# Some constants made on GpSimd, and each output chunk stored by one transfer instead of two

## The chip, the cores and the metric

The kernel runs on one core of a Trainium2 chip. The core has five engines with instruction queues of their own: TensorE (PE in the profile, with its weight loads as PEld), VectorE (DVE), ScalarE (ACT), GpSimd (POOL) and SyncE (SP), and 16 DMA engines that the queues of SP, ACT and GpSimd share. The metric is the device time of one execution in microseconds (us). One execution was also taken by the profiler; its span is the time from the first to the last recorded work on the core.

## The reference

The reference is a Nystromformer attention followed by a multiplicative feed-forward layer. All inputs are fp32.

```
A  = sm(q, k_lm); Bm = sm(q_lm, k_lm); C = sm(q_lm, k)      # 8 batches, 8 heads, 576 x 64; 32 landmarks
Z  = Bm^T / (norm1 * norminf);  six times: Z = 2 Z - Z Bm Z
x  = (A Z C v), heads side by side                           # 4608 x 512
h  = (x @ w1) * (x @ w2) @ w3                                # 512 -> 1024 -> 1024
out = h @ w_out                                              # 4608 x 512
```

`sm` is a softmax over the last axis with the scale 1/8, and `q_lm`, `k_lm` are means over groups of 18 rows.

## The kernel before

**Stages.** At the start w3 and w_out are folded into one matrix `w34` (8 row blocks of 128 x 512), each fp32 operand split into a high and a low fp16 part (`fold`, line 505: `split` makes the parts of w_out, `turn` transposes pieces of w3 on PE, `product` multiplies). Then each batch goes through its landmarks, the three score matrices, the inverse, and a projection of `Z C v` through w1 and w2 per head (`project`). `up` (line 451) multiplies this by the normalised scores and forms the product `ab` of the two branches, 128 of the 1024 features at a time. `down` (line 470) multiplies `ab` by `w34`: one chunk of 128 output rows is eight matmuls into the PSUM tile `acc`, and there are 36 chunks, nine for each pair of batches.

**Order.** The order is written out by hand in the string `ORDER`: words are run from left to right, and what each issues is queued on its engines in that order. `F` is one step of the fold, `U..` is `up`, `W0.n` and `W1.n` are the two halves of output chunk n. Waits come from the tiles: a tile that is used in rotation can be written again when its last readers are done.

**The output.** When chunk n is complete, ACT scales it from PSUM into `o_sb` (line 499; 128 x 512 fp32, three buffers in rotation), and SP sends it out in two transfers of 64 partitions (line 502). The rows of a batch are laid out as 64 positions x 9 phases: token 9 p + r of batch b is `rows[b, r, p]`. A unit of 64 partitions is one phase r of one batch, its 64 rows lie 9 rows apart in memory, and a chunk is two units that follow each other: mostly two phases of one batch, and in one chunk of nine the last phase of one batch and the first of the next. The last chunk (n = 35) is computed in two halves of 256 columns, each with an ACT or DVE evacuation (lines 481 and 484) and two transfers, one on SP and one on ACT (line 489). SP's queue also carries the loads of V (lines 126 and 131), the exchange of landmarks between partitions (line 232) and, at the start, pieces of w3 (line 574) and of w_out (line 578).

**The constants.** `constants` (line 162) is called once at the start, after GpSimd was given a copy that waits for a piece of w_out (`gate`, line 603) and eight load issues (lines 107 and 137). It makes, all on DVE: `mask4`, `eye`, `onesq`; `selc`, the 0/1 matrix with which PE spreads the softmax reciprocals over the columns (line 382); `lomask`; `eye2`; `bt`, whose second half holds the identity, used for the squares in line 305; and `xsp`, two zeroed tiles into which line 355 writes the landmark values. On GpSimd the next instruction behind the load issues is the copy in `paced_w3` (line 619), which lets SP send the fifth piece of w3 only once the first batch's k has come.

Of the kernel before, what the change touches and what calls it, by code (L numbers as in the profile page):

```python
# [21 lines left out]
DM = 512  # L22
# [4 lines left out]
RT = 9  # L27
# [40 lines left out]
def kernel(  # L68
# [11 lines left out]
    nc = tc.nc  # L80
# [8 lines left out]
    def big():  # L89
        return psp.tile([128, 2, 512], FP32, name="big", bufs=3)  # L90
# [4 lines left out]
    def acc():  # L95
        return psp.tile([128, 512], FP32, name="acc", bufs=1)
# [58 lines left out]
    for a in range(2):  # L155
        for x in range(2):
            sl = slice(64 * a + 32 * x, 64 * a + 32 * x + 32)
            for ph in range(2):
                c = 64 * a + 32 * ph
                nc.gpsimd.tensor_copy(out=pick[sl, x, c:c + 32], in_=ident[sl, sl])  # L160

    def constants():

        mask4 = consts.tile([128, 4, 32], FP32, name="mask4")
        eye = consts.tile([128, 2, 32], FP32, name="eye")
        onesq = consts.tile([128, 2, 4, 2, 4], FP16, name="onesq")
        nc.vector.memset(mask4, 0.0)
        nc.vector.memset(onesq, 0.0)
        for h in range(4):
            sl = slice(32 * h, 32 * h + 32)  # L170
            nc.vector.memset(mask4[sl, h, :], 1.0)
            for qd in range(2):
                nc.vector.tensor_copy(out=eye[sl, qd, :], in_=ident[sl, sl])
                nc.vector.memset(onesq[sl, qd, :, qd, h:h + 1], 1.0 / X64)

        selc = consts.tile([128, 2, 4, 128], FP16, name="selc")
        lomask = consts.tile([128, 1], FP32, name="lomask")
        selr = consts.tile([128, 8], FP32, name="selr")
        nc.vector.memset(selc, 0.0)
        nc.vector.tensor_tensor(out=selr, in0=eye[:, 0, 0:8], in1=eye[:, 0, 8:16], op=ALU.add)  # L180
        nc.vector.reduce_sum(out=lomask, in_=eye[:, 0, 8:16], axis=AX.X)
        nc.vector.tensor_scalar(out=lomask, in0=lomask, scalar1=-1.0, scalar2=None, op0=ALU.mult)
        for c in range(4):
            sl = slice(32 * c, 32 * c + 32)
            for qd in range(2):
                nc.vector.tensor_copy(
                    out=selc[sl, qd, c, :].rearrange("p (h m) -> p h m", m=32),
                    in_=selr[sl, 4 * qd:4 * qd + 4].unsqueeze(2).to_broadcast([32, 4, 32]),
                )
        eye2 = consts.tile([128, 32], FP32, name="eye2")  # L190
        nc.vector.tensor_tensor(out=eye2, in0=eye[:, 0], in1=eye[:, 0], op=ALU.add)
        bt = consts.tile([128, 4, 64], FP32, name="bt")
        for i in range(4):
            nc.vector.tensor_copy(out=bt[:, i, 32:64], in_=eye[:, 0])
        xsp = [consts.tile([128, 256], FP32, name=f"xsp{i}") for i in range(2)]
        for t in xsp:
            nc.vector.memset(t, 0.0)
        return mask4, eye, eye2, onesq, selc, lomask, bt, xsp


# [265 lines left out]
    rows = out.rearrange("(b p r) f -> b r p f", b=B, r=RT)  # L466

    hold = {}

    def down(n, half):  # L470
        b0, t0 = n // 9 * 2, 128 * (n % 9)
        ab = sts[b0]["ab"]
        if n == 35:
            o_sb = hold["o_sb"] = hold.get("o_sb") or po.tile([128, DM], FP32, name="o_sb")
            c = slice(256 * half, 256 * half + 256)
            pso = acc() if half else big()[:, 0, :]
            for j in range(8):
                nc.tensor.matmul(pso[:, 0:256], ab[:, j, t0:t0 + 128], w34[:, j, c],
                                 start=(j == 0), stop=(j == 7))
            if half == 0:  # L480
                nc.scalar.activation(out=o_sb[:, c], in_=pso[:, 0:256], func=AXF.Copy,
                                     scale=1.0 / (X64 * X64))
            else:
                nc.vector.tensor_scalar(out=o_sb[:, c], in0=pso[:, 0:256],
                                        scalar1=1.0 / (X64 * X64), scalar2=None, op0=ALU.mult)
            for i in range(2):
                u = t0 // 64 + i
                eng = nc.scalar if i else nc.sync
                eng.dma_start(out=rows[b0 + u // RT, u % RT][:, c], in_=o_sb[64 * i:64 * i + 64, c])
            return  # L490
        if half == 0:
            hold["ps"] = big()[:, 0, :] if n > 30 and n % 2 else acc()
        pso = hold["ps"]
        for j in range(4 * half, 4 * half + 4):
            nc.tensor.matmul(pso[:, :], ab[:, j, t0:t0 + 128], w34[:, j, :],  # L495
                             start=(j == 0), stop=(j == 7))
        if half == 1:
            o_sb = po.tile([128, DM], FP32, name="o_sb")
            nc.scalar.activation(out=o_sb, in_=pso, func=AXF.Copy, scale=1.0 / (X64 * X64))  # L499
            for i in range(2):  # L500
                u = t0 // 64 + i
                nc.sync.dma_start(out=rows[b0 + u // RT, u % RT], in_=o_sb[64 * i:64 * i + 64, :])


    def fold(pf, wof, w3f, wsp, warm_up):
# [102 lines left out]
    load_weight(0, moe_w1)  # L608
    load_weight(1, moe_w2)
    mask4, eye, eye2, onesq, selc, lomask, bt, xsp = constants()  # L610
    fd = fold(pf, wof, w3f, wsp, warm_up)
    next(fd)
# [43 lines left out]
    for word in ORDER.split():  # L656
        name, _, b = word.partition(".")
        if name == "F":
            next(fd, None)
        elif name == "P":  # L660
            paced_w3(int(b))
        elif name == "L3":
            load_w3(int(b))
        elif name[0] == "W":
            down(int(b), int(name[1]))
        else:
            b = int(b)
            if name == "U0a":
                if pab is None:
                    for _ in fd:  # L670
                        pass
                    pf_scope.__exit__(None, None, None)
                    pab = ctx.enter_context(tc.tile_pool(name="pab", bufs=2))
                open_ab(b)
            of_batch[name](sts[b], b)
# [30 lines left out]
```

## Time and profile before

| | us |
|---|---|
| median of three runs | 263.78 (263.65 to 267.96) |
| the profiled execution | 263.62 |
| its span | 261.8 |
| first and last chunk evacuated (line 499) | 86.5, 255.9 |
| last matmul ends | 257.59 |
| last store issued on SP | 258.38 |

The page of the profile gives, for each engine, its busy time and share of the span, then the chain of work that ended last, followed back from the end, and then groups of equal instructions with the mean duration of one. A row of the timeline reads: start and duration in us, engine, line and operation, output<-input, shape, count, and in brackets the idle time before it and what ended that. In the list of DMA issues the last number is the median time from issue to landing. Packets are what the DMA engines move one after the other; "under 512 B" counts all packets smaller than that.

### The profile page before, as it was taken

What the parts mean: (1) busy time and instruction counts of PE and PEld (TensorE: products, weight loads), DVE (VectorE), ACT (ScalarE), POOL (GpSimd) and SP (SyncE); (2) the same over time, 40 slices, a digit from 0 to 9 for tenths busy, and PEclk for the clock granted to TensorE, in tenths of its full rate; (3) what the DMA queues carried; (4) which work ended last, traced back from release to release, by engine and by line L of the source; (5) the groups of instructions that cost most, each with busy time, mean ns of one, the idle gap of its engine ahead of it and who ended that gap; (6) DMA issues with size and microseconds to landing.
All of it is one profiled execution on the core that took longest, in us unless ns stands there. A gap on an engine that the chain in (4) does not pass through costs nothing.

```text
span 261.8 us, 10518 instructions
## 1 busy us (share of the span) xinstructions
PE 251.5 (96%) x4578; PEld 148.7 (57%) x4578; DVE 173.8 (66%) x352; ACT 134.7 (51%) x305; POOL 103.2 (39%) x134
## 2 busy tenths in 40 slices
PE   7999999998989999999999999999999999999993
PEld 3455554454556558557654674766476556656642
DVE  8765887556958687788856958767775656464410
ACT  4543236343652565576449546746646555455531
POOL 3630018998981999027092597504400000000000
PEclk9999999999999999999999999999999999999999
DMA  6999998999963448976668496933640713222355
GB/s 236 333 243 284 245 248 191 183 137 240 175 105 50 120 101 167 216 195 114 131 100 162 101 214 150 161 58 86 147 86 3 173 43 80 45 62 61 81 118 127
DMA packets 25070, 37.78 MB, mean 144 GB/s; under 512 B 4672, under 2 KB 13120, under 8 KB 25024
## 3 DMA queue, kind: packets, MB, share of 16 engines
q1 hardware_dynamic: 14704, 24.65, 36.9%
q0 software_dynamic: 9728, 11.54, 28.1%
q10 hardware_dynamic: 592, 0.92, 1.1%
q8 instruction: 36, 0.59, 1.0%
q14 instruction: 10, 0.08, 0.1%
HBM read 38.80 MB, written 9.44 MB: 184 GB/s over the span
## 4 chain that ended last, share of the span: by engine, by line
PE 89%; DVE 4%; ACT 3%; issue 1%; DMA 1%; SPq 0%; DVEq 0%; ACTq 0%
PE big L455 23%; PE acc L495 22%; PE acc L530 14%; PE big L442 5%; PE big L344 5%; PE big L399 4%; PE big L517 2%; PE small L530 2%; PE big L382 2%; PE small L421 2%; PE big L274 1%; PE big L495 1%; PE big L322 1%; DVE ab L461 1%; PE small L248 1%
## 5 line engine op out<-in xcount | busy, mean ns | idle before, releaser
L455 PE MATMUL big<-ahat,gt 128*128 128x288 f16 x512 | 73.1, 287 | 0.7 <-DVE ab L461 0.6
L495 PE MATMUL acc<-w,ab 128*128 128x512 f16 x264 | 67.2, 380 | 0.0
L461 DVE TENSOR_TENSOR ab<-a_sb,big 128x576 f16<-128x576 f16 x64 | 48.0, 750 | 27.2 <-ACT a_sb L459 16.8
L455 PEld LDWEIGHTS <-gt 128*128 128x128 f16 x512 | 48.3, 98 | 21.1 <-issue 3.1
L459 ACT CAST a_sb<-big 128x576 f16<-128x576 f32 x64 | 40.8, 640 | 33.9 <-PE big L455 32.9
L206 POOL TENSOR_TENSOR tr<-qkT 128x1024 f32<-128x1024 f16 x14 | 29.7, 2123 | 70.0 <-DVE qkT L143 69.8
L530 PE MATMUL acc<-wsp,w3t 128*128 128x512 f16 x168 | 41.3, 380 | 0.7 <-ACT w L533 0.5
L495 PEld LDWEIGHTS <-ab 128*128 128x128 f16 x280 | 25.3, 98 | 24.9 <-issue 3.5
L499 ACT ACTIVATE o_sb<-acc 128x512 f32<-128x512 f32 x33 | 19.8, 599 | 19.5 <-PE acc L495 19.1
L530 PEld LDWEIGHTS <-w3t 128*128 128x128 f16 x192 | 18.1, 98 | 18.9 <-issue 1.3
L143 DVE STREAM_TRANSPOSE qkT<-qkn 128x576 uint32<-128x576 uint32 x32 | 24.0, 763 | 2.0 <-DMA qkn<-in_k_dram 2.0
L448 DVE TENSOR_SCALAR gt<-big 128x1024 f16<-128x1024 f32 x16 | 19.1, 1211 | 3.1 <-PE big L442 3.0
L446 ACT ACTIVATE gt<-big 128x1024 f16<-128x1024 f32 x16 | 15.9, 1032 | 5.9 <-PE big L442 5.9
L211 POOL TENSOR_TENSOR tr<-tr 128x512 f32<-128x512 f32 x14 | 17.9, 1282 | 0.6
L442 PE MATMUL big<-wup,zt 64*32 64x512 f16 x512 | 17.4, 380 | 0.2 <-ACT en L282 0.2
L523 DVE SCALAR_TENSOR_TENSOR w3t<-big,w3t 128x512 f16<-128x512 f32 x16 | 11.0, 687 | 10.0 <-ACT w3t L522 10.0
L522 ACT ACTIVATE w3t<-big 128x512 f16<-128x512 f32 x16 | 9.5, 596 | 13.9 <-PE big L517 13.8
L284 DVE STREAM_TRANSPOSE ent<-en 128x576 f32<-128x576 f32 x16 | 12.1, 768 | 4.4 <-ACT en L282 4.4
L344 PE MATMUL big<-vt,ent 64*32 64x64 f32 x1152 | 14.2, 226 | 0.0
L282 ACT ACTIVATE en<-big 128x288 f32<-128x288 f32 x32 | 12.7, 411 | 2.9 <-PE big L274 2.7
L344 PEld LDWEIGHTS big<-vt,ent 64*32 64x32 f32 x1152 | 12.7, 105 | 2.0 <-ACT a_sb L459 0.5
L328 ACT ACTIVATE eat<-big 128x576 f16<-128x576 f32 x16 | 9.6, 652 | 7.3 <-PE big L322 7.3
(214 smaller groups left out, 285.2 us busy)
## 6 DMA issues: line engine op xcount, KB each, us to landing
out_dram<-o_sb SPq DMA_DIRECT2D x70, 128.0 KB, 2.5
vt<-in_v_dram SPq DMA_DIRECT2D x16, 288.0 KB, 5.3
vt<-in_v_dram SPq DMA_DIRECT2D x32, 144.0 KB, 4.0
qkn<-in_k_dram POOLq DMA_DIRECT2D x12, 288.0 KB, 5.4
qkn<-in_q_dram POOLq DMA_DIRECT2D x12, 288.0 KB, 4.9
w3f<-in_moe_w_dram SPq DMA_DIRECT2D x6, 512.0 KB, 6.7
wup<-in_moe_w_dram POOLq DMA_DIRECT2D x4, 512.0 KB, 25.3
wof<-in_moe_w_out_dram SPq DMA_DIRECT2D x6, 256.0 KB, 4.5
```

Source lines behind the costliest of these rows:

```text
L143: nc.vector.transpose(out=st["qkT"][:, t, prs].rearrange("p c r q e -> p (c r q e)").bitcast(U32), in_=st["qkn"][:, t, prs, :].rearrange(" ...
L206: add(out=tr, in0=x[:, :, 0:4, :], in1=x[:, :, 4:8, :], op=ALU.add)
L211: add(out=tr[:, :, 0:2, :], in0=tr[:, :, 0:2, :], in1=tr[:, :, 2:4, :], op=ALU.add)
L344: nc.tensor.matmul(psV[32 * o:32 * o + 32, qd, 0:64], ent[sl, pr, r, :], vt[sl, pr, 64 * r:64 * r + 64], start=(r == 0), stop=(r == RT - 1 ...
L442: nc.tensor.matmul(psG[o:o + 32, qd, :], zt[rs, i, h, :], wup[rs, h, w, fs], start=(i == 0), stop=(i == 1), tile_position=(64 * qd, o))
L448: nc.vector.tensor_scalar(out=g[:, :, w, fs], in0=psG, scalar1=1.0 / ZS, scalar2=None, op0=ALU.mult)
L455: nc.tensor.matmul(p[:, c, 0:HS], st["g"][:, qd, w, 128 * j:128 * j + 128], st["ahat", qd][:, c, :], start=(qd == 0), stop=(qd == 1))
L459: nc.scalar.copy(out=st["a_sb"], in_=p[:, :, 0:HS])
L461: nc.vector.tensor_tensor(out=st["ab"][:, j, st["t0"]:st["t0"] + S].rearrange("p (c s) -> p c s", c=2), in0=st["a_sb"], in1=p[:, :, 0:HS], ...
L495: nc.tensor.matmul(pso[:, :], ab[:, j, t0:t0 + 128], w34[:, j, :], start=(j == 0), stop=(j == 7))
L499: nc.scalar.activation(out=o_sb, in_=pso, func=AXF.Copy, scale=1.0 / (X64 * X64))
L530: nc.tensor.matmul(psW[j][:, :], turned[j, c // 4][:, a, c % 4, :], wsp[:, b, c, :], start=(c == 0 and a + b == 0), stop=(c == 7 and a == 1))
```

## The change

`selc` is zeroed and filled on GpSimd instead of DVE, and so are the identity half of `bt` and the zeros of `xsp`; `selr`, `lomask` and `eye2` stay on DVE. The instructions are the same in kind and number, and stand on GpSimd behind the load issues and ahead of the copy of line 619.

The stores go through a new function `store`. Where both units of a chunk belong to one batch, one transfer takes all 128 partitions of `o_sb` and writes two phases of 64 rows (31 chunks). Where the chunk crosses from one batch to the next, two transfers of 64 partitions stay as they were (four chunks). The last chunk is stored in one transfer for each half of its columns, the first on ACT and the second on SP. In the built program the combined transfer has 128 x 512 elements on the side of `o_sb` and 2 x 64 x 512 on the side of the output, with steps of 512, 4608 and 1 element.

```diff
-        nc.vector.memset(selc, 0.0)
+        nc.gpsimd.memset(selc, 0.0)
...
-                nc.vector.tensor_copy(
+                nc.gpsimd.tensor_copy(
                     out=selc[sl, qd, c, :].rearrange("p (h m) -> p h m", m=32),
                     in_=selr[sl, 4 * qd:4 * qd + 4].unsqueeze(2).to_broadcast([32, 4, 32]),
                 )
...
         for i in range(4):
-            nc.vector.tensor_copy(out=bt[:, i, 32:64], in_=eye[:, 0])
+            nc.gpsimd.tensor_copy(out=bt[:, i, 32:64], in_=eye[:, 0])
...
         for t in xsp:
-            nc.vector.memset(t, 0.0)
+            nc.gpsimd.memset(t, 0.0)
...
+    def store(b, u, o_sb, c, eng):
+        bu, r = b + u // RT, u % RT
+        if r < RT - 1:
+            eng.dma_start(out=rows[bu, r:r + 2][:, :, c], in_=o_sb[:, c])
+            return
+        for i in range(2):
+            eng.dma_start(out=rows[bu + i, (r + i) % RT][:, c], in_=o_sb[64 * i:64 * i + 64, c])
...
-            for i in range(2):
-                u = t0 // 64 + i
-                eng = nc.scalar if i else nc.sync
-                eng.dma_start(out=rows[b0 + u // RT, u % RT][:, c], in_=o_sb[64 * i:64 * i + 64, c])
+            store(b0, t0 // 64, o_sb, c, nc.sync if half else nc.scalar)
...
-            for i in range(2):
-                u = t0 // 64 + i
-                nc.sync.dma_start(out=rows[b0 + u // RT, u % RT], in_=o_sb[64 * i:64 * i + 64, :])
+            store(b0, t0 // 64, o_sb, slice(0, DM), nc.sync)
```

## The prediction

> **What bounds the kernel now.** I read the head of the page first (busy shares), then the chain that ended last, then the DMA part, because half of the change is about stores.
>
> ```profile
> span 261.8 us, 10518 instructions
> ...
> PE 251.5 (96%) x4578; PEld 148.7 (57%) x4578; DVE 173.8 (66%) x352; ACT 134.7 (51%) x305; POOL 103.2 (39%) x134
> ...
> DMA packets 25070, 37.78 MB, mean 144 GB/s; under 512 B 4672, under 2 KB 13120, under 8 KB 25024
> ...
> PE 89%; DVE 4%; ACT 3%; issue 1%; DMA 1%; SPq 0%; DVEq 0%; ACTq 0%
> ...
> out_dram<-o_sb SPq DMA_DIRECT2D x70, 128.0 KB, 2.5
> ```
>
> PE is busy 96% of the span and makes 89% of the chain; DMA has 1% of the chain, the last store. So today nothing done to stores or to constants can win more than a few tenths, but anything that holds PE up is lost time in full. The 70 stores land in 2.5 us each (median) with the output buffer `o_sb` three deep, and a chunk is made every 4.9 us (36 chunks from 86.5 to 257.6 us), so they are far from PE.
>
> The number that I use most is "under 512 B 4672". Before has 196 transfers: 74 stores, 48 of V, 24 exchanges of landmarks, 18 of w3 and w_out, 32 on GpSimd. The exchanges move rows of 256 B, 24 x 64 = 1536 packets. What is left is 4672 - 1536 = 3136 = 196 x 16: each transfer leaves 16 tiny packets, one per DMA engine that took part. **Every transfer of before is cut over 16 engines**, and in each of them the outermost count is 32, 64 or 128 on both sides.
>
> **Part 1, constants.** The start, by the timeline:
>
> ```profile
> 3.14 0.48 DVE L179 MEMSET selc<- 128x512 uint32 x1 [0.15 <-issue]
> ...
> 3.98 1.45 DVE L186 CAST selc<-selr 32x128 f16<-32x128 f32 x8
> ...
> 5.55 0.43 DVE L194 COPY bt<-eye 128x32 f32<-128x32 f32 x4
> ...
> 5.98 0.55 DVE L197 MEMSET xsp<- 128x256 f32 x2
> ...
> 7.72 1.19 PE L530 MATMUL acc<-wsp,w3t 128*128 128x512 f16 x4 [0.22 <-DVE w3t L523]
> ...
> 17.75 0.18 POOL L619 CAST w3f<-qkn 128x1 f32<-128x1 f16 x1 [2.60 <-PE acc L530]
> ...
> 29.25 0.60 PE L517 MATMUL big<-ident,w3f 128*128 128x128 f32 x4
> ```
>
> DVE loses 0.48 + 1.45 + 0.43 + 0.55 = 2.91 us ahead of its first w_out split, which then starts when its input is there (5.34 us) and not at 6.44. PE's only wait on that is the 0.22 us in the row above; before and after it PE works off its own queue. Gain: 0 to 0.2, I take 0.2.
>
> GpSimd gets 15 instructions, behind its eight load issues, which end at 15.15 us. Bounds from its own rows: a 256-element fp16 memset takes 0.31 us and a 128-element fp32 one 0.20, so the memset of 1024 is about 0.97; a 32x32 cast takes 0.20 (1.58 / 8), and 96 elements more cost up to 0.21 by the two-input rate of L211 and L212 (2.15 ns an element), so eight are 1.6 to 3.3; four copies 0.8, two memsets 0.6: 4.0 to 5.7 us, 4.8 in the middle. The pacing copy L619 behind them moves from 17.75 to about 20.0, and with it the fifth 512 KB piece of w3, which SP issues at 17.96 and which takes some 6.7 us to land: 26.9 instead of 24.7. PE transposes that piece at 29.25. Cost 0, with 2.3 us of cover; beyond that it would cost PE us for us, once. The next GpSimd work (38.44) and the first readers of bt (40.2), xsp (60.4) and selc (62.3) are further off.
>
> **Part 2, stores.** 74 issues become 41: 31 of 256 KB and 8 of 128 KB on SP, and two of 128 KB for the last chunk, one on ACT, one on SP. Issuing is shorter (0.57 us each), which only matters at the very end: the last matmul ends at 257.59, DVE's piece at 258.11, and SP sends its second half-piece at 258.38; with one issue it leaves at 258.13. Gain 0.2 to 0.5.
>
> But the new store names its destination as 2 row phases x 64 rows x 512 elements, against 128 partitions on the other side. For the first time a transfer has an outermost count below 16. No row of before shows such a one; the bounds are 16 engines, as all others have, and 2. A cut along the outermost index fits all 196 transfers, and a cut along the flattened rows fits them too. I take 2: dividing the first dimension that an instruction lists is the simpler of the two, and every engine's share in before (2 to 8 whole outermost rows) can be had that way. This is a choice and not a reading, hence the weight of the first rival below.
>
> The Trainium skill, "DMA: Bandwidth & Descriptors", section "Why a DMA increments its semaphore by 16 and not by 1", says that a transfer runs on the largest number of engines up to 16 that divides the slowest dimension of both sides; by it the store runs on 2. The trace agrees as far as it goes (16 for 32, 64 and 128). The same page of the Trainium skill, in "Rules for kernel authors", asks for one 128-partition transfer in place of two halves, which speaks for the change; by that alone the time would be the first rival's.
>
> Price of a 256 KB store on two engines: 64 packets of 2 KB each. Two rows price a packet:
>
> ```profile
> 8.00:9.00 1.00, 1.00 (x6) 0.37 (x5) 1.00 (x3) 0.50 (x1) 0.00 (x1) 1.00 1.05 404
> ```
>
> (window; last two columns are the DMA share of 16 engines and GB/s): loads of full 128 partitions run at 404 / (16 x 1.05) = 24.0 GB/s per engine, 85 ns a packet. And for stores alone, from 210 to 256 us:
>
> ```profile
> DMA packets 1935, 3.26 MB, mean 71 GB/s; under 512 B 384, under 2 KB 384, under 8 KB 1928
> ...
> q1 hardware_dynamic: 1928, 3.16, 32.1%
> ```
>
> 0.321 x 46 us x 16 = 236 us over 1544 data packets, 153 ns. There sixteen engines pull from 64 partitions at once; the trace's packet records have the first packets of such a burst at 81 to 91 ns. Two engines, each on its own 64 partitions, don't crowd like that, so I take 85 and keep 153 as the other end. A store then holds its two engines 64 x 85 ns = **5.4 us** (up to 9.8), where chunks come every 4.9 us and in the tail every 1.7.
>
> Those two engines also carry their sixteenth of all loads. From 86 to 207 us (the loads end there) the three large queues hold 40.4 + 21.1 + 1.4% of 16 engines, 76 us per engine; stores are 41 x 64 x 153 ns / 16 = 25 of it, loads 51.
>
> The sum for one of the two engines from the first store on (87.1 us): 31 x 5.44 = 168.6; eight unchanged half stores, 4 packets each at 153 ns, 4.9; the last chunk 64 rows of 1 KB twice, 5.4; loads 51: 230. It ends at 317, the last landing and the end of the span add about 1.2 (258.38 + 2.2 against 261.8): 318. Outside the span lie 1.8 us (263.62 - 261.8): **320**. This sets the end: with `o_sb` three deep ACT's L499 waits for the store three chunks back, `acc` isn't freed, and PE stands in L495, with all that is queued behind it. V loads and landmark exchanges sit in SP's queue behind such stores, up to three of them, 16 us; their lead in the order is of that size, so I add nothing. The gains of 0.2 and 0.5 vanish in it. The profiled run (263.62) is 0.16 under the median of 263.78, so nothing has to be shifted.
>
> **Rivals.**
> 1. The store is cut over 16 engines whatever its outer count. For it: 196 of 196 have 16. Then PE stays the bound: 263.62 - 0.2 - 0.5 = 262.9, no slower than before. It decides as soon as a store's 128 rows are spread over eight engines or more: 16 packets, 1.4 us at 85 ns, under any spacing of chunks.
> 2. Two engines, but the queues of one engine overlap, so that loads cost the stores nothing (the share of 1.05 in the row above is over 1, and one of 1.17 stands at 10 to 11 us): 87.1 + 168.6 + 4.9 + 5.4 + 1.2 + 1.8 = 269, at most somewhat above, since the last chunks can't be had early. Against it: V loads and stores share one queue.
> 3. Two engines at the store row's 153 ns: 31 x 9.8 = 303.6 in place of 168.6: 455.
> 4. The constants hold up w3 on GpSimd: 2.3 us of cover must go first; a doubling of the 4.8 us would cost 2.5. It goes along with any of the others and changes none.
>
> **How the numbers follow.** Forecast 0.74, rival 1 0.16, rival 2 0.06, rival 3 0.04. 320 is the forecast's. Its own range is 277 to 400 and stands for the 0.74: 76 ns a packet (the best 0.2 us slice of the start moves 430 GB/s on 16 engines) with half of the loads hidden is 277, and 125 ns, or 85 ns with the engines idle in places while PE waits for V or landmarks, is 400; taking in rival 2 the range is 269 to 400 and holds 0.80. A difference under 2% (258.5 to 269.1) is about what a measurement can't tell from none: that is rival 1, 0.15 within and 0.01 faster; slower 0.84.
>
> **What would show it.** The count under 512 B: 3488 without the stores' own (4672 - 74 x 16), plus 8 x 16 and 33 x 2 makes 3682 if two engines work, and 3488 + 41 x 16 = 4144 if sixteen do. The landing time of the stores: 8 to 20 us in place of 2.5. ACT's L499 waiting for `out_dram<-o_sb`, PE in L495 waiting for ACT, PE's share near 80%, POOL's constants at 15 to 20 us. A landing time near 3 us and 4144 make the forecast wrong, and PE waiting for V or landmarks instead of `acc` would make its path wrong.

## The result

The changed kernel takes 313.97 us (median; 313.78 to 315.86), against 263.73 us before. The ratio is 1.193, with a 95% interval of 1.189 to 1.197: 50 us slower, where the prediction had 320 with a range of 269 to 400. The profiled execution is of 313.81 us and has a span of 311.7. Now and then an execution of a kernel runs some per cent longer at a lower clock: the ratios in this document leave such executions out, and the profiled execution of run e3 was one, so no times are read from its profile.

The page of the changed kernel, the lines that answer to those shown of before:

```profile
span 311.7 us, 10483 instructions
...
PE 259.2 (83%) x4578; PEld 151.3 (49%) x4578; DVE 171.1 (55%) x337; ACT 134.7 (43%) x305; POOL 107.2 (34%) x149
...
DMA packets 24079, 37.77 MB, mean 121 GB/s; under 512 B 3682, under 2 KB 12130, under 8 KB 24034
...
PE 57%; DMA 28%; POOL 3%; DVE 2%; ACT 2%; issue 2%; SPq 1%; ACTq 0%; DVEq 0%; POOLq 0%
...
out_dram<-o_sb SPq DMA_DIRECT2D x31, 256.0 KB
```

PE's share fell from 96% to 83%, and DMA, which had 1% of the chain, has 28%. The bytes are the same and the packets below 512 B are exactly the 3682 that two engines for each combined store give. The list of issues has lost its landing time: the view finds none for the transfers of SP in this execution.

Where the 50 us lie can be read from the times at which ACT evacuates the chunks (line 499 before, 504 after). Compared with before, chunk 3 is 0.2 us late, chunk 4 is 7.9, chunk 9 is 8.7, chunk 10 is 12.4, and chunk 12 is 24.1. From there to chunk 30 little is added (25.0). The last whole chunk, 34, is 33.6 us late, and the end of the span 49.9. So there are two losses: **24 us in the middle**, in three steps (at chunks 4, 10 and 12), and **26 us at the end**. Of these 26, some 9 are late chunks, with PE waiting 7.4 us for ACT, and 16 are the time for the last stores to land.

The end, from 262 to 272 us in the DMA view of the changed kernel:

```profile
DMA packets 252, 0.51 MB, mean 51 GB/s; under 512 B 3, under 2 KB 3, under 8 KB 252
...
q1 hardware_dynamic: 252, 0.51, 13.1%
```

Nothing but stores runs there, at 51 GB/s and 13.1% of 16 engines: two engines, 25.6 GB/s each, 80 ns for 2 KB, so 5.1 us for a store of 64 packets on each. In the timeline PE is then held by ACT, which is held by the buffer:

```profile
283.69 0.60 ACT o_sb L504
...
284.31 10.18 DMA out_dram<-o_sb
```

```profile
284.34 3.32 PE L500 MATMUL acc<-w,ab 128*128 128x512 f16 x8 [5.76 <-ACT o_sb L504]
```

(the first two rows are of the chain, start and duration; the third is of PE's timeline, with 5.76 us of waiting.) The middle is another matter. PE's waits in the changed kernel, as total, number and longest, and the chain from 92 to 120 and from 162 to 175 us:

```profile
PE big L322 <- DMA lm<-lm: 9.6, 1, 9.6
PE acc L500 <- ACT o_sb L504: 8.5, 2, 5.8
PE small L248 <- DMA lm<-lm: 5.5, 2, 4.0
```

```profile
92.59 0.60 ACT o_sb L504
...
93.22 20.08 DMA out_dram<-o_sb
...
113.31 0.59 SPq L126
...
114.01 5.11 DMA lm<-lm
...
119.25 0.88 PE small L248 x16
...
162.49 10.87 DMA lm<-lm
...
173.49 1.18 PE big L322 x31
```

PE waits 15.1 us for the exchange of landmarks (`lm<-lm`), and there only 2.7 for `acc`. The wait of 4.0 us that ends at 119.25 (the step at chunk 4) begins with chunk 2's store, which is issued at 93.22 and has landed 20 us later. Only then can SP issue a load of V (line 126), and only behind that the next exchange. In the built program the transfers of SP and ACT take turns on eight semaphores, and each waits until the transfer eight places back has landed; the load of V at 113.31 is eight places behind that store. So a slow store stops SP itself, and what stands behind that place in its queue leaves late, whoever needs it.

The other two steps begin with the output buffer. Rows of the timelines of ACT, PE and SP:

```profile
155.56 0.60 ACT L504 ACTIVATE o_sb<-acc 128x512 f32<-128x512 f32 x1 [3.79 <-DMA out_dram<-o_sb]
...
156.20 1.02 PE L500 MATMUL acc<-w,ab 128*128 128x512 f16 x4 [2.73 <-ACT o_sb L504]
...
157.46 4.93 SPq L126 DMA_DIRECT2D vt<-in_v_dram  x1
```

Chunk 10 is evacuated late because ACT waits for a store to give its buffer back, and PE waits for ACT. Its own store is sent at 156.18, and behind it SP takes 4.93 us to issue one load of V (0.66 is the median of that line before). So the exchange at 162.49 leaves 16 us later than it did before (146.28): chunk 10 is 12.4 us late already, and most of the rest is this one issue. It then takes 10.87 us to land, where 2.9 was the median before. The waits of PE in the middle, 15.1 and 2.7 us, are not the whole of the 24; part of the remainder is the lower clock of the last section.

### The profile page after: what moved, and what is told of

The parts are those of the page before. It is cut to its first block, busy times and chain, and to the rows that moved or that the text cites. A ratio compares the mean times of both kernels' runs of the same rounds, so it can differ in the third digit from the quotient of the medians.

```text
span 311.7 us, 10483 instructions
## 1 busy us (share of the span) xinstructions
PE 259.2 (83%) x4578; PEld 151.3 (49%) x4578; DVE 171.1 (55%) x337; ACT 134.7 (43%) x305; POOL 107.2 (34%) x149
## 2 busy tenths in 40 slices
DMA packets 24079, 37.77 MB, mean 121 GB/s; under 512 B 3682, under 2 KB 12130, under 8 KB 24034
## 3 DMA queue, kind: packets, MB, share of 16 engines
q1 hardware_dynamic: 13744, 24.65, 25.6%
## 4 chain that ended last, share of the span: by engine, by line
PE 57%; DMA 28%; POOL 3%; DVE 2%; ACT 2%; issue 2%; SPq 1%; ACTq 0%; DVEq 0%; POOLq 0%
DMA out_dram<-o_sb 20%; PE acc L500 15%; PE big L455 13%; PE acc L533 10%; DMA lm<-lm 6%; PE big L344 3%; PE big L442 3%; PE big L399 2%; PE big L520 2%; PE small L533 2%; DMA w3f<-in_moe_w_dram 2%; PE big L322 1%; PE big L382 1%; PE small L248 1%; DVE ab L461 1%
## 5 line engine op out<-in xcount | busy, mean ns | idle before, releaser
L500 PE MATMUL acc<-w,ab 128*128 128x512 f16 x264 | 70.3, 394 | 8.5 <-ACT o_sb L504 8.5
L455 PE MATMUL big<-ahat,gt 128*128 128x288 f16 x512 | 74.5, 290 | 0.7 <-DVE ab L461 0.4
L455 PEld LDWEIGHTS <-gt 128*128 128x128 f16 x512 | 49.0, 99 | 22.3 <-issue 4.2
L525 ACT ACTIVATE w3t<-big 128x512 f16<-128x512 f32 x16 | 9.5, 596 | 13.7 <-PE big L520 13.6
L344 PEld LDWEIGHTS big<-vt,ent 64*32 64x32 f32 x1152 | 12.5, 105 | 2.6 <-ACT a_sb L459 0.9
```

Of the source, the lines that this page charges most:

```text
L344: nc.tensor.matmul(psV[32 * o:32 * o + 32, qd, 0:64], ent[sl, pr, r, :], vt[sl, pr, 64 * r:64 * r + 64], start=(r == 0), stop=(r == RT - 1 ...
L455: nc.tensor.matmul(p[:, c, 0:HS], st["g"][:, qd, w, 128 * j:128 * j + 128], st["ahat", qd][:, c, :], start=(qd == 0), stop=(qd == 1))
```

## The experiments

Each run is one change to the kernel named. Lateness is against the profiled execution of before, at chunks 3, 12, 29 and 34 and at the end of the span. Runs e9 and e2 to e4 put rows in other places than the reference has them, as their expectations say; the work is the same. Where GpSimd issues the exchanges (e5, e10, e11), the count falls by 1536: there they are moved in 384 packets of 1 KB, not in 1536 of 256 B.

| run | ratio to before (95%) | under 512 B | late at 3, 12, 29, 34, end (us) |
|---|---|---|---|
| the change | 1.193 (1.189 to 1.197) | 3682 | 0.2, 24.1, 24.5, 33.6, 49.9 |
| e1 constants alone | 1.002 (0.998 to 1.006) | 4672 | 0.5, 0.4, 1.0, 1.0, 1.9 |
| e9 dimensions swapped | 1.003 (1.000 to 1.006) | 4144 | 0.0, 0.1, 0.1, 0.1, 0.6 |
| e2 outermost 16 | 1.006 (1.002 to 1.010) | 4080 | 1.0, 0.7, 1.5, 1.5, 2.2 |
| e3 outermost 8 | 1.019 (1.013 to 1.024) | 3784 | |
| e4 outermost 4 | 1.049 (1.045 to 1.053) | 3636 | 1.3, 2.0, 2.0, 5.2, 13.6 |
| e5 exchanges on GpSimd | 1.140 (1.131 to 1.149) | 2146 | 4.7, 9.7, 14.4, 23.4, 39.5 |
| e6 six buffers | 1.193 (1.187 to 1.200) | 3682 | 2.2, 26.6, 26.7, 26.6, 52.4 |
| e7 early half | 1.099 (1.093 to 1.104) | 4192 | -0.5, 24.7, 26.3, 26.3, 27.2 |
| e8 late half | 1.097 (1.091 to 1.102) | 4162 | 0.1, 0.2, 0.3, 9.2, 25.6 |
| e10 exchanges and V on GpSimd | 1.179 (1.174 to 1.184) | 2146 | 9.0, 15.4, 22.6, 31.1, 47.3 |
| e11 before, exchanges on GpSimd | 1.005 (1.002 to 1.009) | 3136 | 2.9, 2.7, 2.7, 2.7, 2.7 |

**Is it the stores, and which property of them?** First the constants by themselves (e1): the four places of `constants` moved to `nc.gpsimd`, `down` as before.

> The kernel before with the constants moved to GpSimd and the stores left as they were. My theory (the stores alone make the loss): 263.3 to 263.8, POOL's constants done near 19.6 us, under-512 B count 4672 as before. Rival (the constants hold up the fifth piece of w3, or a later reader): PE waits for w3 near 29 us and the time is 265 or more.

264.98 us, no difference that could be measured, and a little above the expected 263.3 to 263.8, as the runs of before on that chip were too (264.74). In the changed kernel GpSimd's constants read:

```profile
15.15 1.04 POOL L179 MEMSET selc<- 128x1024 f16 x1
16.26 2.19 POOL L186 CAST selc<-selr 32x128 f16<-32x128 f32 x8
18.51 0.65 POOL L194 COPY bt<-eye 128x32 f32<-128x32 f32 x4
19.11 0.55 POOL L197 MEMSET xsp<- 128x256 f32 x2
19.62 0.18 POOL L622 CAST w3f<-qkn 128x1 f32<-128x1 f16 x1
```

The pacing copy stands at 19.62, 1.9 us later than before, and PE's transpose of that piece of w3 starts at 28.99: the cover held.

Then the stores. The next run keeps all 41 transfers, their sizes and their addresses, and swaps two dimensions of the destination:

```diff
-            eng.dma_start(out=rows[bu, r:r + 2][:, :, c], in_=o_sb[:, c])
+            eng.dma_start(out=rows[bu, r:r + 2].rearrange("r p f -> p r f")[:, :, c], in_=o_sb[:, c])
```

> The changed kernel with the same 41 transfers to the same addresses, and only the two outer dimensions of the destination swapped: 64 x 2 x 512 instead of 2 x 64 x 512 (within a chunk the rows come in another order than the reference has them). Theory (only the outermost count sets the engines): under-512 B count 3488 + 41 x 16 = 4144, 263.5 to 265.5, equal to the time with 16 x 8 rows. Rival (the scattered addresses of the combined transfer or its size cost by themselves): 275 or more.

265.01 us and a count of 4144, as the theory had it:

```profile
DMA packets 24541, 37.77 MB, mean 144 GB/s; under 512 B 4144, under 2 KB 12592, under 8 KB 24496
```

```profile
out_dram<-o_sb SPq DMA_DIRECT2D x31, 256.0 KB, 2.5
```

(the second line is of its list of issues; the landing time is back.) The order of two dimensions in one access pattern is the whole of the 50 us (to within the 1.6 us of e9's interval); neither the size of the issue nor its scattered addresses has a part that could be measured.

Three runs set the count in between. Each stores every chunk in one issue to `out.rearrange("(p a) f -> a p f", a=N)`, so that N is outermost:

```diff
-            eng.dma_start(out=rows[bu, r:r + 2][:, :, c], in_=o_sb[:, c])
+            eng.dma_start(out=apart[:, p0:p0 + 128 // N, c], in_=o_sb[:, c])
```

> The changed kernel, with every chunk stored in one issue of 128 partitions, but the destination named as 16 x 8 rows instead of 2 x 64. It writes the rows in another order than the reference has them; bytes, issues and row size stay. Theory (the outermost count sets how many of the 16 engines take part): under-512 B count 3488 + 37 x 16 = 4080, no waits of ACT for stores, 262.5 to 263.6. Rival (one large issue is what costs, by its size, its longer hold on the output buffer or on its place in SP's queue, whatever its cut): near 314, count not near 4080.

> As the run with 16 x 8 rows, destination named as 8 x 16 rows (again another row order than the reference). Theory: 8 engines, 16 packets each, 1.4 us a store at 85 ns a packet; under-512 B count 3488 + 37 x 8 = 3784; 262.5 to 264.5. Rival (the size of the issue): near 314.

> As before, destination named as 4 x 32 rows (another row order than the reference). Theory: 4 engines, 32 packets each, 2.7 us a store; under-512 B count 3488 + 37 x 4 = 3636. Chunks come every 4.9 us on average, so the middle is free of it, but the last five come every 1.7 us: about 1 us is lost on each, 265 to 271. Rival (the size of the issue): near 314. Rival (any store on fewer than 16 engines stalls the landmark exchanges behind it): 275 or more, with PE waiting for the exchanges as in the changed kernel.

The counts are 4080, 3784 and 3636, each to the packet what N engines for a transfer give (3488 + 37 N), and the times rise as N falls: ratios of 1.006, 1.019, 1.049, and 1.193 for the change's 2. All three times lie above the expectations: 265.84 us for 16 (not 262.5 to 263.6, with 264.74 for before on that chip), 269.2 and 270.0 for 8 (two executions; not 262.5 to 264.5), and 277.61 for 4 (not 265 to 271). The time for 4 lies in the range of the rival of stalled exchanges, but its sign is missing: PE waits for no exchange there, and 11.6 of the 13.6 us are added after chunk 29. A store on four engines was taken at 2.7 us, but in the crowded stretch from 252 to 264 us those four move 70 GB/s, 17.5 each or 117 ns a packet, 3.7 us a store. Why four engines are each slower than two was not tried. What follows from this set is the count of engines; the price of a packet in between does not follow from the ends.

**Two losses, or one?** The combined transfer was used for one half of the chunks alone: chunks 0 to 17 in e7, 18 to 35 in e8; the others went out in two transfers of 64 rows.

```diff
-        if r < RT - 1:
+        if whole and r < RT - 1:        # whole: n < 18 in e7, n >= 18 in e8
```

> The changed kernel with the combined transfer for chunks 0 to 17 alone; chunks 18 to 35 are stored in two transfers of 64 rows. Theory A (the loss has two parts, stuck exchanges in the middle, 24 us, and the drain at the end, 26 us): 284 to 291, with PE waiting for exchanges as in the changed kernel and no drain. Rival B (total work of the two engines): half of the stores, and the second half of the run has room to take up what is left, so 264 to 275.

> The changed kernel with the combined transfer for chunks 18 to 35 alone; chunks 0 to 17 are stored in two transfers of 64 rows. Theory A: chunks up to 18 as before the change, the drain at the end stays: 284 to 294. Rival (the drain is only what the stuck middle has pushed to the end): 264 to 275.

290.53 and 289.77 us. The losses of the two add up to those of the change (26.7 + 26.0 against 50.2), so neither takes the other's place. The early half has the exchanges' waits and no drain, the late half has the drain and not one wait for an exchange:

```profile
PE big L322 <- DMA lm<-lm: 10.4, 1, 10.4
PE small L248 <- DMA lm<-lm: 5.7, 2, 4.2
PE acc L500 <- ACT o_sb L504: 1.5, 1, 1.5
```

(PE's waits in e7)

```profile
PE acc L500 <- ACT o_sb L504: 5.6, 1, 5.6
```

(the longest in e8). With that, rival B of e7 falls, a sum over the whole run in which one half takes up what the other has left: in e7 the last 18 chunks go out in ordinary stores, the two engines have room, and nothing is won back, for PE is busy 48.95 of the 50 us from 207 to 257. That the two engines have no time to spare within the half that has the combined stores is not excluded by this; the DMA view of the change, in the section on the prediction, points that way.

**What holds the middle up?** The exchanges were issued by GpSimd, in the changed kernel (e5) and in the kernel before (e11), and with the loads of V of batches 1 to 7 besides (e10).

```diff
-                nc.sync.dma_start(out=halves[ph, a, :, :, 1 - ph, :], in_=halves[1 - ph, a, :, :, 1 - ph, :])
+                nc.gpsimd.dma_start(out=halves[ph, a, :, :, 1 - ph, :], in_=halves[1 - ph, a, :, :, 1 - ph, :])
```

> The changed kernel with the 24 landmark exchanges issued by GpSimd instead of SP, so that they stand behind no store, neither in SP's queue nor in a queue of a DMA engine. Theory A (of the loss of 50 us, the 24 us up to chunk 12 are PE waiting for exchanges that are stuck behind stores, and the two engines have idle time there): PE's waits for exchanges go, the chunks up to 18 are made at most 6 us later than before the change, and the time is 285 to 300, since the last stores still drain on two engines. Rival B (the total work of the two engines sets the time wherever PE waits): 310 to 316 as for the changed kernel.

> The kernel before with only the exchanges moved to GpSimd: the price of the move by itself, for the run in which the changed kernel had it. Theory: 263.5 to 266. Rival (the move itself costs several us, so that the 14 us left there are partly its own): 267 to 275.

> The changed kernel with the landmark exchanges and the V loads of batches 1 to 7 both issued by GpSimd, so that SP holds the stores alone after the start. Theory A (the 14 us that stay in the middle when only the exchanges are moved are V loads behind stores): chunks up to 18 at most 6 us later than before the change, then the drain: 288 to 295. Rival C (they come from the two engines being slow for every transfer that crosses them, whatever its queue): 298 to 305 as with the exchanges alone. Rival D (GpSimd itself becomes late with the 72 issues): over 305, with landmarks late on POOL.

e5 came to 302.4 us, 12 less than the change, just above the range of theory A and below that of rival B. PE's waits for exchanges are gone, and the lateness at chunk 12 is 9.7 us in place of 24.1. But it grows to 14.4 by chunk 29, where theory A allowed 6, and e11 says that the move itself costs 1.5 us of that (265.71 to 264.21). In e5's chain a load of V and stores stand in the place of the exchange (a load of k too, before chunk 4, and twice ACT waiting for an output buffer, at 150.29 and 187.64):

```profile
156.27 2.79 SPq L126
159.12 11.83 DMA vt<-in_v_dram
```

e10 was to show whether V is the rest, and doesn't: 311.26 us, in the range of rival D, late by 15.4 at chunk 12 and 22.6 at chunk 29. The 42 loads bring a load of their own: GpSimd is busy for 144 us (107 in the change), and DVE waits 8.7 us for loads of k in place of 2.8. So the exchanges are shown to be a part of some 10 to 14 us of the middle loss. For the rest, V behind stores and the output buffer are what the chain of e5 names; they were not separated. Theory A also held that the two engines have idle time in the middle. The packet records show little: from the first packet of a store to the last, fewer than two packets were in flight for 5.2 us in the change and for 1.8 us in e5. So why the two engines are done some 12 us earlier in e5 stays open for the larger part.

**Would more buffers help?** Six output buffers in place of three, from a pool opened when the fold's tiles are given up:

```diff
-            o_sb = po.tile([128, DM], FP32, name="o_sb")
+            o_sb = pout[0].tile([128, DM], FP32, name="o_sb")
```

> The changed kernel with six output buffers instead of three. Theory A (the end is set by what two engines can store, 80 to 85 ns a packet): PE is done earlier, by up to 10 us, but the last store lands where it did, 308 to 318. Rival (three buffers are too few for slow stores, and the wait of ACT for a buffer is what costs): 295 or less.

315.54 us: no gain. PE no longer waits for a buffer, the step at chunk 10 is gone (11.1 us late at chunk 9 and at chunk 11), and chunk 34 is evacuated 26.6 us late in place of 33.6. The end of the span, though, is 52.4 us late, 2.5 more: what PE saves is added to the drain, which goes on at 52 GB/s. The end is what two engines can store. The middle is, if anything, worse (26.6 at chunk 12; the wait for the exchange is 13.4 in place of 9.6).

No run is faster than before. With 16 engines the single issue saves nothing that could be measured (e9, e2), and the constants neither.

## Why the prediction was right, and where not

**The cut over two engines** was the step that decided, and it was a choice between two readings that before could not tell apart. e9 with its pair, the change, settles it: same bytes, same addresses, 4144 and 265 us against 3682 and 314. "A cut along the flattened rows" (rival 1) is out. What rival 1 forecast for 16 engines, 262.9, is what such kernels come near (265.0 with 264.2 for before), except that its gain of 0.7 us isn't there. Its condition, eight engines or more, was a little too mild: with eight (e3) the ratio is 1.019, from two executions. The Trainium skill, "DMA: Bandwidth & Descriptors", section "Why a DMA increments its semaphore by 16 and not by 1", had the rule, the largest number up to 16 that divides both sides' slowest dimension; the counts for 2, 4, 8, 16 and 64 agree to the packet.

**The price of a store**, 5.4 us at 85 ns a packet, measured 5.1 at 80 ns in the drain, where nothing else runs. Rival 3 (153 ns) is out. One reading behind the choice was wrong: the first packets of a burst of stores are not all at 81 to 91 ns. In the burst of before at 88.3 us, three of the first sixteen packets of 2 KB take 87 or 88 ns and the others up to 173. The row of the loads, 85 ns, bore the choice alone. The other reading, that 153 ns came from sixteen engines crowding on 64 partitions, fits e9: there the stores of 128 partitions land in 2.5 us for twice the bytes, and the largest queue's share from 210 to 256 us is 20.8% where before had 32.1% for the same stores.

**The sum** came out 6 us high (320 to 314). Its picture, two engines busy almost without a gap from the first store on, is what the DMA view of the changed kernel shows. Two engines of sixteen are 12.5%, a digit of 1; the rows are 87 to 207 us and 207 to 262 us in 40 slices each:

```profile
DMA  2411799915246917323983111583275013882322
...
DMA  5792121111111115561111114521111111111111
```

One slice of eighty lies below. In the packet records fewer than two packets were in flight for 5.2 of the 221.5 us between the first packet of a store and the last. All packets from 86.5 us on that aren't a store's come to 51.7 us when shared over 16 engines, where the sum had 51. So the term that was mis-sized is the price of a packet: at the measured 80 ns the same sum gives 310, 4 us too few, and idle time, which it put at nothing, is of that size. That the two errors go opposite ways is luck, the picture is not. What the records can't show is whether one of the two engines idled while others worked, as they name no engine.

**The path** is the step that failed, though the number didn't suffer by it: "V loads and landmark exchanges sit in SP's queue behind such stores, up to three of them, 16 us; their lead in the order is of that size, so I add nothing". Their lead was not enough: PE waited 15.1 us for exchanges in the change, half of the loss was made in that stretch, and e5 took 12 us of it back. The prediction had the wait of 16 us (the chain shows 20) but not that a transfer's place in a rotation of semaphores, and an issue of 4.93 us, would stop SP's whole queue. It named "PE waiting for V or landmarks instead of `acc`" as what would make its path wrong, and in the middle that is what happened for the most part. The path by `o_sb`, ACT and `acc` holds at the end, from chunk 30 on, and for one step in the middle (PE's 2.7 us at chunk 10). The sum counts the two engines' work and not PE's waits, and these engines had stores to work off whatever PE waited for, so little was missing from it.

**The constants**: cost 0, as predicted; 4.5 us on GpSimd for an estimate of 4.8 (4.0 to 5.7). Rival 4 is out. The gain of 0.2 us at the start isn't seen in e1 (1.002, 0.998 to 1.006). The 0.2 to 0.5 us at the very end by one issue in place of two would lie within e9's interval, but e9 shows no gain (1.003, 1.000 to 1.006).

**Rival 2** (loads beside the stores for nothing, 269) is out: the time is 45 us above it. At 80 ns a packet it would be 259, 55 us under the measured time, where the loads' share is 51.7.

## What to carry to other kernels

Look at the outermost count of both sides of each transfer before joining two of them: here 2 x 64 rows went over two engines, 64 x 2 rows over sixteen, and the order of these dimensions cost 50 us. The count of packets under 512 B tells it from the page alone, 16 for each transfer that is spread fully. A slow transfer costs also through what stands behind it (24 of the 50 us here lie in the middle, where PE waited mostly for exchanges), so ask of each one who shares its queue and its place in a rotation of semaphores, not only who reads its data.

## What was not expected of the hardware

The clock that TensorE is granted falls to half while PE stands, and stays there for some time after. Windows of the changed kernel around the wait for the exchange at 163 to 173 us, the columns being length, busy time of the five engines, granted clock, DMA share and GB/s:

```profile
163.00:168.00 5.00, 0.90 (x85) 0.80 (x72) 1.15 (x3) 0.00 (x0) 4.69 (x6) 0.98 0.82 174
168.00:173.00 5.00, 0.00 (x0) 0.00 (x0) 0.00 (x0) 0.00 (x0) 2.92 (x5) 0.50 0.29 88
173.00:176.00 3.00, 2.51 (x36) 1.19 (x37) 0.00 (x0) 1.19 (x2) 0.00 (x0) 0.50 0.69 215
176.00:179.00 3.00, 3.00 (x18) 2.00 (x17) 0.76 (x2) 0.64 (x1) 0.00 (x0) 0.66 0.80 229
179.00:182.00 3.00, 3.00 (x24) 2.12 (x24) 2.31 (x4) 1.55 (x3) 0.00 (x0) 1.00 0.14 47
```

In half-microsecond and one-microsecond windows of the same trace the clock falls at about 167.8, 3.9 us after PE stopped, and is back at about 178.0, 4.5 us after PE began again. PE's busy time grew from 251.5 to 259.2 us for the same 4578 matmuls, so some of the loss is this and not the waits themselves; how much was not separated, and the prediction left it out. The Trainium skill, "TensorE: Matmul & The Clock Gate", section "What's actually happening", has the half rate after about 3.4 us of idle time and the full one after about as much work; the windows, with 3.9 and 4.5 us, are near both.

Four engines moved 17.5 GB/s each in the tail of e4, two moved 25.6 in that of the change. And the same 128 output rows took a third less DMA time as one transfer of 128 partitions than as two of 64 (20.8% against 32.1% of the engines), with no effect on the time, as nothing waited for it.
